# FFT filter with a bilinear layer on one core: the first transform's tiles alternate between two sets of buffers

## The chip, the cores and the metric

One core of a Trainium2 chip. The time is the device time of one execution, in microseconds (us); the number for the kernel before is the median of three runs.

## The reference

```python
X = np.fft.rfft(x, axis=1)              # x: (8, 3072, 256)
Y = X * (filt_r + 1j * filt_i)[None]
y = np.fft.irfft(Y, n=3072, axis=1)
t = y.reshape(8 * 3072, 256)
return (t @ w_a) * (t @ w_b) @ w_out    # 256 -> 1536 -> 256
```

Eight batches of 3072 positions by 256 channels are filtered in the frequency domain along the positions, and each position then goes through a bilinear layer.

## The kernel before, in words

**The mathematics.** The transform of length 3072 = 128 x 24 is done in four steps of small matmuls: a first transform over 128 positions for each of 24 residues (`s1`, lines 355 to 365, two residues a step, so 12 steps a batch), a second over the 24 with the filter (`s2`, `cross`, `sum_y`, `split_y`, lines 412 to 443, 16 steps a batch), an inverse over 24 (`is1`, line 445), and an inverse over 128 (`is2`, line 544, two calls for each of six chunks of a batch). Between the steps the data goes through DRAM: the first transform stores `zh` and `zl` (`store_z`, lines 367 to 372, three DMAs a step from step 8 on, two before), the filter step loads `zt` (line 398), `is1` stores `td`, and `load_t` (line 537) loads `tt` and `gt`.

**Precision.** Operands are split in a rounded high part and a rest, and a product is made of three matmuls (high by high, high by low, low by high). The split of a tile is always the same pair of instructions: ScalarE (ACT) casts into the high part, and GpSimd (POOL), or VectorE (DVE) where the source is in PSUM, subtracts it to get the low part. For the first transform these are `xh` and `xl` (lines 351, 352, from the loaded `xt`) and `zh` and `zl` (lines 363, 364, from PSUM).

**The main loop and its slots.** `pair` (line 611) is the bilinear layer for two blocks of 128 hidden features: seven products by a Strassen-like scheme (`term`, 6 matmuls each, lines 582 to 584, in the PSUM tiles ps_p, ps_q, ps_r), copies of partial sums by ACT (`held_sum`, line 623), sums by DVE (line 627), the product g (lines 649, 652, 661), its split into gh and gl (`parts`, lines 590, 591) and the output projection (`project`, 24 matmuls a pair, lines 601 to 603). Without other work a pair is 66 matmuls. There are 6 pairs a chunk and 36 a batch. In a pair there are two places, called slots here, at which other work is put in: `hooks(plan, 2p)` ahead of term 3 and `hooks(plan, 2p+1)` behind term 4. So a batch has 72 slots, and while batch b is in the bilinear layer, its slots carry the transforms of batch b+1. The order on every engine is the order in which the program issues the instructions.

**What stands in which slot.** For batch 0, while it makes the first transform of batch 1, a step i begins in slot 12 + i: the split of x in slot 13 + i, the matmuls `s1` in slot 14 + i, `store_z` in slot 15 + i. So each of the slots 15 to 25 holds, in this order, the store of one step, `s1` of the next with the load of a table, the split of x of the one after it, and a load of x two steps ahead:

```python
at(t + 1 if b == 0 else t + 2, split_x, b + 1, i)
    at(t + 1 if b == 0 else t + 2, load_x, b + 1, i + 2)
at(t + 2 if b == 0 else t + 3, s1, b + 1, i)
at(t + 3 if b == 0 else t + 4, store_z, b + 1, i)
```

In the later batches a step begins in every second slot (t = 2i). Slots 17 and 19 of batch 0 also hold `is2` (lines 548 to 557), slot 20 also `load_t` and the first `x_parts`, slot 21 the second (`x_parts`, lines 566, 567, splits the input of the bilinear layer into xoh and xol). The filter steps begin in slot 29 in every batch.

**Buffers.** The tiles of the first transform and of the filter step come from one pool, `later`, each under a tag of its own: xh, xl, zh, zl with one buffer each, xt and st with two, yh, yl, y, v with one each. All of xh, xl, zh, zl, yh, yl, y and v have the same size, 128 x 512 elements of four bytes. An instruction that writes a tile waits until everything has been done that reads the tile before it in the same buffer; for zh and zl those readers are the DMAs of `store_z`. All DMAs named here are issued on the queue of SP, in the program's order.

Of the kernel before, what the change touches and what calls it, by code (L numbers as in the profile page):

```python
# [10 lines left out]
F32R = mybir.dt.float32r  # L11
# [7 lines left out]
B, S, D, DFF = 8, 3072, 256, 1536  # L19
# [177 lines left out]
def fft_filter_bilinear_kernel(ctx: ExitStack, tc, x, filt, fny, wa, wb, wo, s1c, gc, fc, fl, ic, sc, s1f, ff, fi, out):  # L197
# [14 lines left out]
    later, moe = [], []  # L212
# [129 lines left out]
    def load_s(b, i):  # L342
        st = later[0].tile([128, 2, 2, 128], F32R, name="st", tag="st", bufs=2)
        nc.sync.dma_start(out=f32(st), in_=s1d[i])
        held["s", b, i] = st

    def split_x(b, i):
        xt = held.pop(("x", b, i))
        xh = later[0].tile([128, 2, D], F32R, name="xh", tag="xh", bufs=1)
        xl = later[0].tile([128, 2, D], F32R, name="xl", tag="xl", bufs=1)  # L350
        nc.scalar.copy(out=xh, in_=xt)
        nc.gpsimd.tensor_tensor(out=xl, in0=xt, in1=f32(xh), op=ALU.subtract)
        held["xs", b, i] = xh, xl

    def s1(b, i):
        (xh, xl), st = held.pop(("xs", b, i)), held.pop(("s", b, i))
        ps = ps_f.tile([128, 2, D], F32, name="ps", tag="ff")
        for n in range(2):
            for q, (w, m) in enumerate(((0, xh), (0, xl), (1, xh))):
                nc.tensor.matmul(ps[:, n], st[:, n, w], m[:, n], start=q == 0, stop=q == 2)  # L360
        zh = later[0].tile([128, 2, D], F32R, name="zh", tag="zh", bufs=1)
        zl = later[0].tile([128, 2, D], F32R, name="zl", tag="zl", bufs=1)
        nc.scalar.copy(out=zh, in_=ps)
        nc.vector.tensor_tensor(out=zl, in0=ps, in1=f32(zh), op=ALU.subtract)
        held["zs", b, i] = zh, zl
# [305 lines left out]
    with tc.manual_schedule():  # L671
# [60 lines left out]
        for b in range(B):  # L732
# [14 lines left out]
            if b + 1 < B:  # L747
# [5 lines left out]
                for i in range(NI):  # L753

                    t = o + i if b == 0 else 2 * i
                    at(t + 1 if b == 0 else t + 2, split_x, b + 1, i)
                    if i + 2 < NI:
# [3 lines that stand above are left out]
                    if i + 2 < NI:  # L761
                        at(t + 2 if b == 0 else t + 3, load_s, b + 1, i + 2)
                t = 26 if b == 0 else 28
# [4 lines left out]
                for i in range(NJ):  # L768
                    t = 29 + 2 * i
# [8 lines left out]
            for c in range(NC):  # L778
                nb, ncx = (b, c + 1) if c + 1 < NC else (b + 1, 0)
                if nb < B:  # L780
                    t = 12 * c + 5 if c + 1 < NC else 67
# [60 lines left out]
```

## Time and profile before

| | us |
|---|---|
| median of 3 runs | 2687.28 (2687.25 to 2687.7) |
| the profiled execution | 2686.96 |
| its span, first to last instruction | 2685.2 |
| TensorE (PE) busy | 2590.9 (96%) |
| VectorE (DVE) busy | 1667.8 (62%) |
| ScalarE (ACT) busy | 1411.5 (53%) |
| GpSimd (POOL) busy | 1321.5 (49%) |
| mean granted TensorE clock | 0.984 of 2.4 GHz |

A row of a timeline gives the start, the duration, the engine, the line of the kernel, the operation and its tiles; in brackets stands how long the engine had been idle before it and what ended the idle time. A row of waits gives the engine and line that waited, what it waited for, the sum in us, how often, and the longest. Matmuls overlap: each is shown with some 0.28 us, but they start about 0.12 us apart.

### The profile page before, as it was taken

To read this page: it belongs to the slowest core of one execution; us is meant where nothing else is said; L and a number is where in the kernel's file an instruction comes from. 1 tells how busy PE (TensorE), PEld (TensorE's weight loads), DVE (VectorE), ACT (ScalarE), POOL (GpSimd) and SP (SyncE) were. 2 spreads that over 40 slices of the span, in tenths; PEclk is the share of its full clock that TensorE was granted. 3 is DMA by queue.
4 is the path that set the end of the run, shared out by engine and by line. 5 is a ranking of instruction groups with operands and counts; after the bars stand their busy time and mean duration, and the time that the engine had idled before them with its cause. 6 is when DMAs were issued, how large, how long until landed. Compare 5 with 4: busy or idle time off the path is not lost.

```text
span 2685.2 us, 54082 instructions
## 1 busy us (share of the span) xinstructions
PE 2590.9 (96%) x20920; PEld 2521.5 (94%) x20920; DVE 1667.8 (62%) x2648; ACT 1411.5 (53%) x2630; POOL 1321.5 (49%) x1044
## 2 busy tenths in 40 slices
PE   4687999999999999999999999999999999999999
PEld 2387999999999999999999999999999999999999
DVE  5773686457855588456874578654885558744443
ACT  3454455555555555555555555555555555544444
POOL 3564454554545455455544545454454545534333
PEclk6899999999999999999999999999999999999999
DMA  7624442345423443244432444134441444311000
GB/s 247 179 97 156 158 145 70 111 138 153 139 64 123 153 140 108 77 135 159 137 93 83 156 144 141 53 127 155 135 130 61 138 147 143 97 39 32 29 21 17
DMA packets 213635, 310.88 MB, mean 116 GB/s; under 512 B 21393, under 2 KB 121298, under 8 KB 213330
## 3 DMA queue, kind: packets, MB, share of 16 engines
q1 hardware_dynamic: 184882, 278.85, 32.6%
q10 hardware_dynamic: 28496, 28.58, 3.5%
q8 instruction: 164, 2.69, 0.4%
q14 instruction: 93, 0.76, 0.1%
HBM read 202.49 MB, written 108.00 MB: 116 GB/s over the span
## 4 chain that ended last, share of the span: by engine, by line
PE 87%; POOL 4%; DVE 3%; DMA 3%; issue 2%; ACT 1%; SPq 0%; ACTq 0%; POOLq 0%; DVEq 0%
PE po L603 10%; PE ps_p L582 9%; PE ps_p L584 9%; PE ps_p L583 9%; PE po L601 9%; PE po L602 9%; PE ps_r L584 5%; PE ps_r L582 5%; PE ps_r L583 5%; PE ps L548 3%; PE ps_q L582 2%; PE ps_q L584 2%; PE ps_q L583 2%; PE ps L360 2%; PE ps L407 2%
## 5 line engine op out<-in xcount | busy, mean ns | idle before, releaser
L591 POOL TENSOR_TENSOR gl<-g,gh 128x512 fp32r<-128x512 f32 x576 | 748.4, 1299 | 959.0 <-ACT gh L590 891.1
L601 PE MATMUL po<-woh,gh 128*128 128x256 f32 x2304 | 656.9, 285 | 0.0
L603 PE MATMUL po<-woh,gl 128*128 128x256 f32 x2304 | 650.4, 282 | 3.1 <-POOL gl L591 1.1
L590 ACT CAST gh<-g 128x512 fp32r<-128x512 f32 x576 | 359.0, 623 | 551.0 <-DVE g L649 527.4
L602 PE MATMUL po<-wol,gh 128*128 128x256 f32 x2304 | 646.5, 281 | 0.0
L627 DVE TENSOR_TENSOR cs<-ps_r,s 128x512 f32<-128x512 f32 x288 | 199.1, 691 | 448.5 <-PE ps_r L584 395.0
L623 ACT COPY s<-ps_p 128x512 f32<-128x512 f32 x576 | 338.0, 587 | 240.4 <-PE ps_p L584 203.8
L603 PEld LDWEIGHTS po<-woh,gl 128*128 128x128 f32 x2304 | 434.3, 188 | 7.8 <-POOL gl L591 7.8
L601 PEld LDWEIGHTS po<-woh,gh 128*128 128x128 f32 x2304 | 435.8, 189 | 3.1
L602 PEld LDWEIGHTS po<-wol,gh 128*128 128x128 f32 x2304 | 435.5, 189 | 2.9
L582 PE MATMUL ps_p<-xoh,wah 128*128 128x256 f32 x1152 | 326.9, 284 | 29.9 <-ACT s L623 16.5
L584 PE MATMUL ps_p<-xol,wbh 128*128 128x256 f32 x1152 | 324.2, 281 | 0.0
L583 PE MATMUL ps_p<-xoh,wal 128*128 128x256 f32 x1152 | 323.9, 281 | 0.0
L584 PE MATMUL ps_p<-xol,wah 128*128 128x256 f32 x1152 | 323.4, 281 | 0.0
L582 PE MATMUL ps_p<-xoh,wbh 128*128 128x256 f32 x1152 | 323.0, 280 | 0.0
L583 PE MATMUL ps_p<-xoh,wbl 128*128 128x256 f32 x1152 | 322.8, 280 | 0.0
L627 DVE TENSOR_TENSOR cs<-ps_q,s 128x512 f32<-128x512 f32 x288 | 199.1, 691 | 182.9 <-PE ps_q L584 158.5
L649 DVE TENSOR_TENSOR g<-cs 128x512 f32<-128x512 f32 x288 | 301.3, 1046 | 5.6 <-POOL gl L591 5.6
L567 POOL TENSOR_TENSOR xol<-xf,xoh 128x256 fp32r<-128x256 f32 x192 | 245.7, 1300 | 21.3 <-ACT xoh L566 21.3
L661 DVE TENSOR_TENSOR g<-ps_p,cs 128x256 f32<-128x256 f32 x288 | 122.1, 424 | 213.9 <-ACT cs L660 211.2
L442 POOL TENSOR_TENSOR yl<-y,yh 128x512 fp32r<-128x512 f32 x112 | 144.2, 1288 | 223.8 <-ACT yh L441 223.8
L582 PEld LDWEIGHTS ps_p<-xoh,wah 128*128 128x128 f32 x1152 | 217.5, 189 | 33.1 <-ACT s L623 18.2
(125 smaller groups left out, 6241.5 us busy)
## 6 DMA issues: line engine op xcount, KB each, us to landing
filt<-in_filt SPq DMA_DIRECT2D x336, 128.0 KB, 2.8
z<-zh SPq DMA_DIRECT2D x112, 256.0 KB, 2.9
zt<-z SPq DMA_DIRECT2D x112, 256.0 KB, 3.0
td<-t ACTq DMA_DIRECT2D x128, 192.0 KB, 2.2
out<-ot SPq DMA_DIRECT2D x95, 256.0 KB, 2.1
tt<-td SPq DMA_DIRECT2D x47, 512.0 KB, 4.2
xt<-in_x SPq DMA_DIRECT2D x84, 256.0 KB, 2.8
st<-s1d SPq DMA_DIRECT2D x84, 256.0 KB, 3.4
```

The source lines that it names most:

```text
L567: nc.gpsimd.tensor_tensor(out=xl[:, o], in0=xf[:, i], in1=f32(xh[:, o]), op=ALU.subtract)
L582: nc.tensor.matmul(o, wh[:, p, w], xh[:, i], start=first and h == 0, stop=False, skip_group_check=True)
L583: nc.tensor.matmul(o, wl[:, p, w], xh[:, i], start=False, stop=False, skip_group_check=True)
L584: nc.tensor.matmul(o, wh[:, p, w], xl[:, i], start=False, stop=True, skip_group_check=True)
L590: nc.scalar.copy(out=gh, in_=g[:, f])
L591: nc.gpsimd.tensor_tensor(out=gl, in0=g[:, f], in1=f32(gh), op=ALU.subtract)
L601: nc.tensor.matmul(o, gh[:, ts], woh[:, n], start=n == 0 and j % 2 == 0, stop=False, skip_group_check=True)
L602: nc.tensor.matmul(o, gh[:, ts], wol[:, n], start=False, stop=False, skip_group_check=True)
L603: nc.tensor.matmul(o, gl[:, ts], woh[:, n], start=False, stop=n == NF - 1, skip_group_check=True)
L623: nc.scalar.copy(out=s, in_=bank)
L627: nc.vector.tensor_tensor(out=cs[:, :, n], in0=bank, in1=s, op=ALU.add)
L649: nc.vector.tensor_tensor(out=g[:, 0].rearrange("p (t n) -> p t n", t=2), in0=cs[:, 0, 0:2], in1=cs[:, 1, 0:2], op=ALU.mult)
```

## The change

The four tiles of a step of the first transform are taken from the tags xh, xl, zh, zl when i is even and from yh, yl, y, v, the tags of the filter step, when i is odd. Nothing else is changed: the same instructions and DMAs in the same order, and the same tags with the same number of buffers in the pool.

```diff
+    SHARED = ("xh", "xl", "zh", "zl"), ("yh", "yl", "y", "v")
+
     def split_x(b, i):
         xt = held.pop(("x", b, i))
-        xh = later[0].tile([128, 2, D], F32R, name="xh", tag="xh", bufs=1)
-        xl = later[0].tile([128, 2, D], F32R, name="xl", tag="xl", bufs=1)
+        xh, xl = (later[0].tile([128, 2, D], F32R, name=n, tag=t, bufs=1) for n, t in zip(("xh", "xl"), SHARED[i % 2][:2]))
...
-        zh = later[0].tile([128, 2, D], F32R, name="zh", tag="zh", bufs=1)
-        zl = later[0].tile([128, 2, D], F32R, name="zl", tag="zl", bufs=1)
+        zh, zl = (later[0].tile([128, 2, D], F32R, name=n, tag=t, bufs=1) for n, t in zip(("zh", "zl"), SHARED[i % 2][2:]))
```

## Rows read from the trace of the kernel before

**Rows 1.** Busy time by stretches: us, busy us of each engine, clock, DMA share, GB/s.
```profile
195.00:285.00 90.00, 73.42 (x569) 71.80 (x567) 33.72 (x58) 39.22 (x77) 38.94 (x31) 0.94 0.51 166
285.00:375.00 90.00, 88.45 (x721) 86.89 (x722) 69.77 (x103) 48.84 (x92) 42.84 (x33) 1.00 0.45 138
```
**Rows 2.** Costliest groups of TensorE, 206.2 to 286.9 us: busy, mean ns | idle before.
```profile
L582 PE MATMUL ps_p<-xoh,wah 128*128 128x256 f32 x24 | 8.1, 336 | 18.0 <-ACT s L623 13.3 <-DVE cs L627 4.8
```
**Rows 3.** Waits of ACT, 206 to 287 us; the whole execution gives the same row.
```profile
ACT zh L363 <- DMA z<-zh: 29.2, 9, 5.1
```
**Rows 4.** Timelines of ACT, POOL and SP's queue, one step of the first transform.
```profile
222.42 0.58 ACT L363 CAST zh<-ps 128x512 fp32r<-128x512 f32 x1 [3.46 <-DMA z<-zh]
...
223.60 1.27 POOL L352 TENSOR_TENSOR xl<-xt,xh 128x512 fp32r<-128x512 f32 x1 [4.16 <-ACT xh L351]
...
224.89 0.38 SPq L339 DMA_DIRECT2D xt<-in_x  x1
225.33 0.46 SPq L369 DMA_DIRECT2D z<-zh  x1
...
228.81 0.58 ACT L363 CAST zh<-ps 128x512 fp32r<-128x512 f32 x1 [2.31 <-DMA z<-zh]
```
**Rows 5.** Timeline of TensorE: first transform matmul, first stall, last stall.
```profile
206.22 0.28 PE L360 MATMUL ps<-xh,st 128*128 128x256 f32 x1
...
213.93 0.28 PE L584 MATMUL ps_r<-xol,wbh 128*128 128x256 f32 x1
217.37 0.38 PE L582 MATMUL ps_p<-xoh,wah 128*128 128x256 f32 x1 [3.16 <-ACT s L623]
...
286.46 0.40 PE L582 MATMUL ps_p<-xoh,wah 128*128 128x256 f32 x1 [1.67 <-ACT s L623]
```
**Rows 6.** Busy time by stretches, columns as in rows 1, where the clock falls.
```profile
226.00:230.00 4.00, 4.00 (x23) 4.00 (x23) 1.00 (x2) 1.69 (x5) 1.28 (x2) 0.58 0.84 259
258.00:266.00 8.00, 5.66 (x36) 5.66 (x37) 2.60 (x5) 4.99 (x10) 5.63 (x5) 0.79 0.39 122
274.00:278.00 4.00, 4.00 (x23) 4.00 (x24) 0.49 (x1) 1.63 (x4) 1.88 (x2) 0.61 0.77 260
```
**Rows 7.** Timeline of TensorE: the matmuls of one is2 call.
```profile
239.34 1.06 PE L548 MATMUL ps<-gt,tt 128*128 128x128 f32 x8
```
**Rows 8.** Timelines of ACT and TensorE in slot 14, whose cast waits for no DMA.
```profile
207.13 0.59 ACT L363 CAST zh<-ps 128x512 fp32r<-128x512 f32 x1 [0.34 <-PE ps L360]
...
209.77 0.31 PE L582 MATMUL ps_p<-xoh,wah 128*128 128x256 f32 x1
```
**Rows 9.** Timelines of ACT and SP's queue around slot 20, step 6.
```profile
247.91 0.59 ACT L363 CAST zh<-ps 128x512 fp32r<-128x512 f32 x1 [2.30 <-DMA z<-zh]
...
251.80 0.43 SPq L369 DMA_DIRECT2D z<-zh  x1
...
257.66 0.58 ACT L363 CAST zh<-ps 128x512 fp32r<-128x512 f32 x1 [5.08 <-DMA z<-zh]
```
**Rows 10.** Timeline of POOL in slot 20.
```profile
250.33 2.43 POOL L567 TENSOR_TENSOR xol<-xf,xoh 128x256 fp32r<-128x256 f32 x2
```
**Rows 11.** Two stretches as in rows 1, and landing of the DMAs of zh.
```profile
206.20:286.90 80.70, 62.66 (x477) 61.04 (x476) 30.34 (x52) 33.58 (x67) 33.45 (x27) 0.94 0.54 173
...
270.00:280.00 10.00, 7.42 (x51) 7.22 (x49) 3.04 (x5) 4.29 (x8) 3.61 (x3) 0.83 0.66 219
...
DMA to landing us min/median/max: 2.4/3.4/5.8
```
**Rows 12.** Waits of TensorE from 285 us to the end.
```profile
PE ps_r L584 <- POOL xol L567: 2.5, 7, 0.4
```
**Rows 13.** Line 649 from 195 to 285 us: duration ns min/median/max.
```profile
L649 DVE TENSOR_TENSOR g<-cs x7: 681/681/1252, 200.7 to 280.1; 128x512 f32<-128x512 f32 x7
```
**Rows 14.** Timelines of SP's queue and DVE: last store of step 11, first y.
```profile
289.93 0.45 SPq L372 DMA_DIRECT2D z<-zh  x1
...
300.25 0.74 DVE L418 SCALAR_TENSOR_TENSOR y<-ps,sct,filt 128x512 f32<-128x512 f32 x1
```

## The prediction

> **What bounds the kernel now.** I read the busy time by stretches first. Before and after the first transform of batch 1 TensorE is busy nearly all the time; in 195 to 285 us it is busy 73.4 of 90 us at a mean clock of 0.94, and in the next 90 us 88.5 at 1.00 [rows 1]. So time can be won only in that stretch. Who ends TensorE's idle time there is the second view: 18.0 us before matmuls into ps_p, released by ACT's copy of s or by DVE's sums [rows 2]. Both engines take their work in order, so the third view asks what ACT itself waited for: its cast into zh waited 29.2 us, nine times, for the DMA that stores the zh of the step before [rows 3]. The whole execution has the same sum in the same nine, so the casts of the other batches, where a step comes only every second slot, wait for no store.
>
> The fourth view is one turn of the loop [rows 4]: cast zh of step 2 at 222.42, then xh of step 3, then POOL's xl from 223.60 for 1.27, then SP issues the load of x (it waits for that xl, since xt has two buffers), and only behind it on SP the store of zh at 225.33, 2.91 us after the cast. It lands when ACT goes on, at 228.81: 3.48 us. One turn is 6.39 us. TensorE's own work for one slot is shorter: 30 matmuls pass from 206.22 [rows 5] to 209.77 [rows 8], of which the last shows 0.03 of waiting, so 0.1173 us each; a pair with two transform steps has 66 + 12 = 78, so 9.15 us, 4.6 us a slot. The store's round trip sets the pace, not TensorE.
>
> **What the stage costs above TensorE's work.** From the first transform matmul (206.22) to the matmul that ends the last stall (286.46) are 80.24 us [rows 5]. Between them lie the rest of pair 7 (36 matmuls), five pairs of 66, the first 18 of pair 13 and 72 of the transform: 456 x 0.1173 = 53.5 us. Two is2 calls come to it, of about 0.95 us each (the row's 1.06 holds the tail of its last matmul) [rows 7]. That makes 55.4; the excess is 24.8 us. It has three parts: 18.0 idle [rows 2]; the clock, which falls from 2.4 to 1.2 GHz in three spells behind stalls [rows 6] and loses 0.42 x 4 + 0.21 x 8 + 0.39 x 4 = 4.9 us; and about 0.16 us at each of eight restarts (217.37 - 213.93 - 0.118 = 3.32 against 3.16 shown as idle [rows 5]), 1.3 us. 18.0 + 4.9 + 1.3 = 24.2, near the 24.8.
>
> **What the change does.** Steps with odd i take the buffers of yh, yl, y, v. No instruction or DMA is added, dropped or moved. Waits change:
>
> Removed: zh(i) no longer waits for the store of zl and zh(i-1), but for that of i-2. That store is issued 2.91 us after its cast and lands 3.48 later, 6.4 us after it [rows 4]; the next cast into the same buffer comes two slots, 9.15 us, after it. So some 2.8 us are spare. xh and xl alternate too; that is worth nothing, since xh(i) follows zh(i-1) on ACT, which waits for the matmuls that read xh(i-1).
>
> Added: the filter step's first y waits for the store of step 11, its yh for s1's matmuls five slots earlier, and step 1 of a batch for the filter step of the batch before, ten or more slots back. For y the margin is on view: last store issued at 289.93, first y at 300.25 [rows 14]; the longest landing of zh is 5.8 us [rows 11]. Queued behind that y on DVE are the pair's sums, on which TensorE waits; they cost nothing as long as those 10.3 us cover the landing. Cost 0, bounds 0 and a rival below.
>
> **What stays late.** In even slots nothing is spare: cast zh at 207.13, then zl and two sums on DVE, then term 4's matmul at 209.77, which shows 0.31 instead of 0.28 [rows 8]; a late zh passes on one for one. In odd slots the copy of s comes behind zh and xh, and TensorE has 30 matmuls, 3.5 us, before it needs that copy done. The cast of zh starts 0.9 us behind the slot's first matmul (206.22 [rows 5], 207.13 [rows 8]) and lasts about 0.6, xh and s the same, so 2.7; some 0.8 us is spare. So I look at even steps. Step 8: in the slot of step 6 the loads of tt and gt stand ahead of the store, which is issued at 251.80, 3.89 after the cast at 247.91, and lands 5.86 later [rows 9]; 9.75 against 9.15 leaves 0.6 us. Step 10: step 8 is the first whose zh is stored twice and its store comes behind a late xl; 0.4, my choice between 0 and the 2.4 us by which the longest landing exceeds the median [rows 11]. POOL: the pair with x_parts gives it two xl (1.27 each [rows 4]), two gl of much the same size and four xol, two of which take 2.43 [rows 10]: about 10.0 us in a pair of 9.15. I count 0.6 of that as reaching TensorE, about two waits of the size that TensorE has for xol elsewhere (2.5 us in 7) [rows 12]. Sum 1.6. Bounds: 0 (every wait covered), and 12 us (five even steps, each late by 2.4).
>
> **Sum.** 24.8 - 1.6 = 23.2 us. Behind the stage TensorE is at its limit [rows 1] and each later step has its place in the slots, so the gain reaches the end whole. The profiled execution took 2686.96 us, 0.3 under the median of the runs shown, 2687.28. That makes 2663.8 for it, and as a median **2664.1**. The matmul of 286.46 would come near 263.
>
> **A row that speaks against it.** Of the seven products g (L649) in the stage the longest took 1.25 us, where POOL's xol ran beside it, the others 0.68 [rows 13]. With the stalls gone POOL's work lies closer. If every pair paid this, 7 x 0.57 = 4.0 us more; I take none, since between g and the project matmuls that use it lie more than 2 us of other TensorE work. The Trainium skill, SBUF — State Buffer, section "SBUF: two separate sides", says that a DVE operation with two SBUF inputs and a GpSimd operation exclude each other for a whole instruction; by that each such meeting would be paid in full, and the 1.25 against 0.68 agrees.
>
> **Rivals.**
> (a) The DMA engines become the bound. They are busy 0.54 of 80.7 us at 173 GB/s, 14.0 MB [rows 11]. In 55.4 us that is 253 GB/s and a share of 0.78. For it: the busiest ten microseconds of the stage moved 219 GB/s [rows 11]. At that rate 14.0 MB take 64 us: gain 80.2 - 64 = 16, 2671. Against it: single 4 us stretches moved 259 and 260 [rows 6], and the engines pause in every turn now.
> (b) POOL and DVE lock each other out in every pair as above: gain 23.2 - 4.0, 2668.
> (c) The change doesn't uncouple the steps: the buffers alternate, but SP still puts each store behind the load that waits for xl, so a turn remains near 6.4 us and the stall moves from zh to another wait. For it: that order is untouched. Against it: with zh free, xl follows the matmuls, not the store. Gain 0 to 5, 2685.
> (d) Slower: y of each filter step holds DVE until the store of step 11 has landed. It decides from a landing of 10.3 us in batch 1; to eat the 23.2 us it must come 3.3 us late in each of seven batches. With one more landing of 5.8 each time, 7 x 5.8 = 41: 2664 + 41 = 2705. Against it: the load of the filter step's input already waits for that same store.
> (e) Many small waits, as in the upper bound: gain 24.8 - 12, 2674.5.
>
> **How the numbers follow.** Forecast 0.72, (a) 0.10, (b) 0.04, (e) 0.06, (c) 0.05, (d) 0.03. A change of 0.2%, 5.4 us, is about what a measurement of this kernel can tell from none. Faster: 0.72 + 0.10 + 0.04 + 0.06 = 0.92; same 0.05; slower 0.03. The range runs from the whole excess with a microsecond of reading error, 2661.5, to the bound of 12 us, 2674.5; it holds the forecast, (a), (b) and (e).
>
> **What would show it.** Right: in the changed profile ACT's wait of zh for the DMA falls from 29.2 to under 3 us; TensorE's idle time before ps_p falls from 18 to under 3; the clock stays at 1.00 through the stage; the same matmul that ended the stage at 286.46 comes near 263; the DMA share rises to about 0.78 with landings below 6 us. Wrong: landings over 6.2 us (9.15 - 2.91), a turn still near 6.4 us, or DVE waiting at y.

## The result and the profile after

The changed kernel takes 2662.84 us (median of six runs, 2660.59 to 2663.57), the kernel before 2687.2 us in the same comparison (six runs, 2683.71 to 2687.7). The ratio is 0.9911, with a 95% interval of 0.9898 to 0.9923: 24.4 us less, between 21 and 27. The forecast was 2664.1 with a range of 2661.5 to 2674.5.

The profiled execution took 2662.36 us, 24.6 less than that of before. First its busy time by stretches (us, busy us of PE, PEld, DVE, ACT and POOL, clock, DMA share, GB/s), the same stretch as in [rows 1], then the stage from its first transform matmul to the matmul that ended the last stall, as in [rows 11]:

```profile
195.00:285.00 90.00, 89.95 (x758) 89.56 (x758) 47.84 (x83) 50.95 (x97) 46.88 (x37) 1.00 0.58 194
...
205.40:261.90 56.50, 56.45 (x476) 56.15 (x475) 30.12 (x52) 34.24 (x66) 33.80 (x28) 1.00 0.74 245
```

TensorE is busy throughout and its clock never falls. The waits of TensorE from 205 us to the end, all of them:

```profile
PE ps_r L584 <- POOL xol L567: 2.5, 7, 0.4
PE po L603 <- POOL gl L591: 1.1, 2, 0.7
PE ps L405 <- DMA zt<-z: 0.2, 1, 0.2
```

The 18.0 us before ps_p [rows 2] are gone. Of ACT's nine waits of zh [rows 3] one is left (waits of ACT, 205 to 262 us):

```profile
ACT zh L363 <- DMA z<-zh: 1.1, 1, 1.1
```

One cast to the next, in the timelines of ACT and SP's queue; these are steps 2, 3 and 4, and the first and the last of them use the same buffer:

```profile
215.58 0.59 ACT L363 CAST zh<-ps 128x512 fp32r<-128x512 f32 x1 [0.84 <-PE ps L361]
...
218.53 0.46 SPq L369 DMA_DIRECT2D z<-zh  x1
...
219.88 0.58 ACT L363 CAST zh<-ps 128x512 fp32r<-128x512 f32 x1 [0.20 <-PE ps L361]
...
225.73 0.58 ACT L363 CAST zh<-ps 128x512 fp32r<-128x512 f32 x1 [0.85 <-PE ps L361]
```

The store still leaves 2.95 us behind its cast (218.53 - 215.58), as in [rows 4]. But the cast of step 3 no longer waits for it: it comes 4.30 us behind that of step 2, and what ended ACT's idle time is TensorE (PE ps L361), not a DMA. Step 4, which does need that store to have landed, comes 10.15 us behind step 2, with an is2 call in between. The ends of the stage on TensorE:

```profile
205.42 0.28 PE L361 MATMUL ps<-xh,st 128*128 128x256 f32 x1
...
261.76 0.28 PE L582 MATMUL ps_p<-xoh,wah 128*128 128x256 f32 x1
```

That is 56.34 us against 80.24 [rows 5]: 23.9 us of the 24.6. The rest lies outside the stage, which begins at 205.42 instead of 206.22. Nothing in the change touches that part, and over the profiled runs of all eleven kernels the beginning lies anywhere from 203.91 to 206.95.

### The profile page after: what moved, and what is told of

Read it like the earlier page. It is cut to its first block, busy times and chain, and to the rows that moved or that the text cites. A ratio compares the mean times of both kernels' runs of the same rounds, so it can differ in the third digit from the quotient of the medians.

```text
span 2660.6 us, 54030 instructions
## 1 busy us (share of the span) xinstructions
PE 2589.5 (97%) x20920; PEld 2518.2 (95%) x20920; DVE 1665.2 (63%) x2648; ACT 1412.2 (53%) x2630; POOL 1321.8 (50%) x1044
## 4 chain that ended last, share of the span: by engine, by line
PE 88%; POOL 4%; DVE 3%; issue 2%; DMA 2%; ACT 1%; SPq 0%; ACTq 0%; POOLq 0%; DVEq 0%
PE po L603 10%; PE ps_p L582 10%; PE ps_p L583 9%; PE ps_p L584 9%; PE po L601 9%; PE po L602 9%; PE ps_r L584 5%; PE ps_r L582 5%; PE ps_r L583 5%; PE ps L548 3%; PE ps_q L582 2%; PE ps_q L584 2%; PE ps_q L583 2%; PE ps L361 2%; POOL xol L567 2%
```

## The experiments

All comparisons are with the kernel before, run on the same chip.

**Which tiles carry the gain.** Four kernels, all from the kernel before, alternate only some of the four tiles.

The run z_only alternates zh and zl.

```diff
-        zh = later[0].tile([128, 2, D], F32R, name="zh", tag="zh", bufs=1)
-        zl = later[0].tile([128, 2, D], F32R, name="zl", tag="zl", bufs=1)
+        zh = later[0].tile([128, 2, D], F32R, name="zh", tag=("zh", "y")[i % 2], bufs=1)
+        zl = later[0].tile([128, 2, D], F32R, name="zl", tag=("zl", "v")[i % 2], bufs=1)
```

> Only zh and zl alternate (with y and v); xh and xl keep one buffer each. Theory (the whole loss is the cast into zh and the subtraction into zl waiting for the store of the step before): all of the gain, 2662 to 2665 us, ACT's waits of zh for the store about 1 us in one step. Rival (the alternation of xh and xl lets POOL and ACT run ahead and carries part of it): 5 us or more of the gain is missing, 2668 or above.

Measured: 2661.58 us, ratio 0.9912 (0.9897 to 0.9926). All of the gain.

The run x_only alternates xh and xl.

```diff
-        xh = later[0].tile([128, 2, D], F32R, name="xh", tag="xh", bufs=1)
-        xl = later[0].tile([128, 2, D], F32R, name="xl", tag="xl", bufs=1)
+        xh = later[0].tile([128, 2, D], F32R, name="xh", tag=("xh", "yh")[i % 2], bufs=1)
+        xl = later[0].tile([128, 2, D], F32R, name="xl", tag=("xl", "yl")[i % 2], bufs=1)
```

> Only xh and xl alternate (with yh and yl); zh and zl keep one buffer each. Theory: nothing, 2686 to 2688 us, ACT still waits some 29 us for the store of zh. Rival: part of the gain, 2680 or below.

Measured: 2686.51 us, ratio 1.0003 (0.9994 to 1.0012). ACT's waits in its stage (200 to 295 us) still show

```profile
ACT zh L363 <- DMA z<-zh: 26.6, 8, 4.9
```

so half of the change, the two x tiles, does nothing here.

The run zh_only alternates zh alone.

```diff
-        zh = later[0].tile([128, 2, D], F32R, name="zh", tag="zh", bufs=1)
+        zh = later[0].tile([128, 2, D], F32R, name="zh", tag=("zh", "y")[i % 2], bufs=1)
```

> Only zh alternates; zl keeps one buffer. Theory: ACT's wait goes, but DVE's subtraction into zl now waits for the store of zl, which lands half a microsecond behind that of zh. In odd slots DVE has room, in even slots it stands ahead of the sums that TensorE needs: some 1.3 us in each of six even slots, 7 to 8 us of loss left, 2668 to 2676. Rival (ACT's order alone is what hurts): the whole gain, 2663 to 2665. Second rival (both tiles have to be free for any gain): 2685 or above.

Measured: 2668.74 us, ratio 0.9939 (0.9924 to 0.9953): two thirds of the gain. Its waits from 200 to 290 us, of DVE, of ACT and of TensorE:

```profile
DVE zl L364 <- DMA z<-zl: 31.4, 10, 5.6
...
ACT s L623 <- DVE cs L627: 10.3, 4, 3.9
```

```profile
PE ps_p L582 <- ACT s L623: 6.0, 3, 2.4
PE ps_p L582 <- DVE cs L627: 3.0, 4, 1.8
```

The wait has gone from ACT to DVE in nearly its old size, and of 31.4 us on DVE 9.0 reach TensorE. The size was as expected, the place not quite: I had put all of it in even slots, by way of DVE's sums; 6.0 of it came by way of the copy of s in odd slots. That copy was late because it had to wait for a DVE sum (10.3 us in four), and the sum stood behind the late zl.

The run zl_only alternates zl alone.

```diff
-        zl = later[0].tile([128, 2, D], F32R, name="zl", tag="zl", bufs=1)
+        zl = later[0].tile([128, 2, D], F32R, name="zl", tag=("zl", "v")[i % 2], bufs=1)
```

> Only zl alternates; zh keeps one buffer. Theory: the cast of zh still waits for the store in every step and everything behind it follows, so no gain: 2684 to 2688 us. Rival (DVE's half of the wait counts for itself): 2680 or below.

Measured: 2685.69 us, ratio 0.9999 (0.9989 to 1.0008). With zh still waiting (31.6 us in ten steps on ACT) a second buffer for zl is worth nothing. So the two do not add: zl alone is worth 0, zh alone 17, both together 24.

**Where in the run the gain lies.**

The run z_batch1 alternates zh and zl in the transform of batch 1 alone.

```diff
-        zh = later[0].tile([128, 2, D], F32R, name="zh", tag="zh", bufs=1)
-        zl = later[0].tile([128, 2, D], F32R, name="zl", tag="zl", bufs=1)
+        zh = later[0].tile([128, 2, D], F32R, name="zh", tag=("zh", "y")[i % 2 if b == 1 else 0], bufs=1)
+        zl = later[0].tile([128, 2, D], F32R, name="zl", tag=("zl", "v")[i % 2 if b == 1 else 0], bufs=1)
```

> zh and zl alternate only in the transform of batch 1; the later six batches keep one buffer. Theory (all the loss is in the stage of batch 1, where a step comes every slot): the whole gain, 2662 to 2665 us. Rival (some of the gain is spread over the later batches): 2666 or above.

Measured: 2662.47 us, ratio 0.9911 (0.9897 to 0.9926). Twelve steps of one batch hold the whole gain; the other 72 steps lose nothing with one buffer.

**Is it the buffer, or the store's way to DRAM?** Two kernels move the place of the store among the slots; the second also moves the first loads of the filter step.

The run store_early is the kernel before with this edit:

```diff
-                    at(t + 3 if b == 0 else t + 4, store_z, b + 1, i)
+                    at(t + 2 if b == 0 else t + 4, store_z, b + 1, i)
```

> The kernel before, with one buffer each, but in batch 0 the store of a step is issued right behind its first transform, ahead of the loads of the table and of x of that slot, instead of behind them. Theory (what hurts is the store's whole round trip, of which 2.9 us are its place on SP's queue behind a load that waits for xl): the store leaves about 1.4 us behind the cast instead of 2.9 and the wait shrinks by 1.5 us in each of eleven steps; a turn falls from 6.4 to about 4.9 us against the 4.6 that TensorE needs. Most of the gain without a second buffer: 2664 to 2673 us. Rival (only a second buffer helps, the place on the queue is worth nothing): 2685 or above.

Measured: 2662.83 us, ratio 0.9914 (0.9899 to 0.9928). The same gain with one buffer each, more than I had expected. The timelines of ACT and SP's queue, and the landing of the DMAs of zh from 195 to 290 us (min/median/max):

```profile
210.18 0.38 SPq L339 DMA_DIRECT2D xt<-in_x  x1
...
212.00 0.59 ACT L363 CAST zh<-ps 128x512 fp32r<-128x512 f32 x1 [0.24 <-ACT cs L660]
...
212.61 0.32 SPq L369 DMA_DIRECT2D z<-zh  x1
...
216.89 0.59 ACT L363 CAST zh<-ps 128x512 fp32r<-128x512 f32 x1 [0.83 <-PE ps L360]
...
DMA to landing us min/median/max: 2.0/2.6/6.0
```

The store leaves 0.61 us behind the beginning of the cast, when the cast is just done, where I had put 1.4: nothing on SP stands ahead of it. It also lands in 2.6 us in the middle instead of 3.4 [rows 11]. I put that down to the load of x, which is issued 2.43 us before the store here and 0.44 us before it in [rows 4]; no run changes this alone. 0.6 + 2.6 = 3.2 us fits into a slot of 4.6, and ACT waited for the store only 2.8 us in two steps. The larger wait is that of step 8: the store of step 7 leaves behind the loads of tt and gt and lands some 6.0 us later, and TensorE loses 1.35 us, its only wait in this stage (timelines of SP's queue, ACT and TensorE):

```profile
242.14 0.32 SPq L369 DMA_DIRECT2D z<-zh  x1
...
248.18 0.59 ACT L363 CAST zh<-ps 128x512 fp32r<-128x512 f32 x1 [2.37 <-DMA z<-zh]
...
250.79 0.39 PE L582 MATMUL ps_p<-xoh,wah 128*128 128x256 f32 x1 [1.35 <-DVE cs L627]
```

The run store_late is the changed kernel with this edit:

```diff
-                    at(t + 3 if b == 0 else t + 4, store_z, b + 1, i)
+                    at(t + 4, store_z, b + 1, i)
...
-                t = 26 if b == 0 else 28
+                t = 28
```

> The changed kernel, two sets of buffers, but in batch 0 each store is issued one slot later (and the first loads of the filter step two slots later, as in all other batches). Theory (the pace is set by the time from a cast to the landing of its store against the time to the next cast into the same buffer): the store now leaves behind the load of x of the slot after, 2.9 us behind the next cast, lands 3.5 later, and the cast two steps on cannot come before: a turn of 6.4 us a step, as in the kernel before, so nearly the whole gain is lost: 2683 to 2689 us. Rival (two buffers are enough, wherever the store stands): 2663 to 2666.

Measured: 2685.73 us, ratio 0.9999 (0.999 to 1.0009). Two sets of buffers, and nothing is left of the gain. ACT's timeline has the old turn, 6.27 and 6.28 us from cast to cast:

```profile
229.66 0.58 ACT L363 CAST zh<-ps 128x512 fp32r<-128x512 f32 x1 [3.97 <-DMA z<-zh]
235.93 0.58 ACT L363 CAST zh<-ps 128x512 fp32r<-128x512 f32 x1 [2.15 <-DMA z<-zh]
242.21 0.59 ACT L363 CAST zh<-ps 128x512 fp32r<-128x512 f32 x1 [1.64 <-DMA z<-zh]
```

Not all of the loss is this turn, though. From the first transform matmul (203.91) to the matmul that stood at 286.46 before (here 278.69) are 74.78 us, against 80.24 in the kernel before and 56.34 in the changed kernel: 18.4 of the 23.9 us are lost in the stage. The rest is lost behind it, where TensorE waits 3.73 us for the load of the filter step's input and then runs at half clock for some 6 us, which costs 3.1 more (timeline of TensorE, and busy time from that matmul on):

```profile
278.69 0.39 PE L582 MATMUL ps_p<-xoh,wah 128*128 128x256 f32 x1 [2.30 <-ACT s L623]
...
295.41 0.58 PE L405 MATMUL ps<-zt,fct 128*128 128x256 f32 x1 [3.73 <-DMA zt<-z]
...
295.41:301.70 6.29, 6.19 (x27) 5.90 (x28) 1.92 (x3) 0.62 (x2) 0.00 (x0) 0.50 0.62 185
```

No run separates what of this second wait comes from the later stores and what from the later loads of the filter step. So the turn is shown for some three quarters of the loss; that the total met the expected range owes the rest to a wait that I had not foreseen.

**Both remedies at once.**

The run both is the changed kernel with this edit:

```diff
-                    at(t + 3 if b == 0 else t + 4, store_z, b + 1, i)
+                    at(t + 2 if b == 0 else t + 4, store_z, b + 1, i)
```

> The changed kernel with the store also issued early as in the run store_early. Theory (in the changed kernel only step 8 still waits, 1.1 us in all on ACT): that wait goes, and with it 0.3 us of TensorE's time: the same as the changed kernel within 1 us, 2661 to 2664. Rival (the order on SP matters more than that, because loads of x now come later): 2665 or above.

Measured: 2662.13 us (2661.39 to 2662.63), ratio 0.991 (0.9895 to 0.9925). No cast waits for a store any more, but the time lies within the runs of the changed kernel. No wait of TensorE is left in the stage, which takes 55.98 us here (206.53 to 262.51).

**How much room have the DMA engines?**

The run extra_stores is the changed kernel with two more stores a step in batch 1, to a scratch tensor that nothing reads:

```diff
+    junk = drc.tile([128, 4 * NI, D], F32, name="junk")
...
+        if b == 1:
+            for k in range(2):
+                nc.sync.dma_start(out=junk[:, 4 * i + 2 * k:4 * i + 2 * k + 2], in_=f32(zh))
```

> The changed kernel with two more stores of zh to a place of its own in each of the twelve steps of batch 1, 6.3 MB on top of 14.0 in the stage of 56 us; the stores lengthen the time that zh is held. Theory (the DMA engines, at a share of 0.74 and 243 GB/s in the stage, have little room left): 20.3 MB at some 290 to 320 GB/s take 63 to 70 us, so the stage grows by 7 to 14 us: 2670 to 2677. Rival (the engines still have ample room, the double buffer hides it): 2663 to 2665.

Measured: 2667.81 us, ratio 0.9931 (0.9915 to 0.9948): 5 us slower than the changed kernel, so neither side's range held it. Its waits of ACT and TensorE in the stage, TensorE's two stalls, and four stretches of busy time (columns as above):

```profile
ACT zh L364 <- DMA junk<-zh: 5.2, 2, 3.3
...
PE ps_p L586 <- DVE cs L631: 3.0, 2, 2.3
...
219.29 0.39 PE L586 MATMUL ps_p<-xoh,wah 128*128 128x256 f32 x1 [0.74 <-DVE cs L631]
251.52 0.38 PE L586 MATMUL ps_p<-xoh,wah 128*128 128x256 f32 x1 [2.25 <-DVE cs L631]
```

```profile
210.00:220.00 10.00, 9.26 (x79) 9.06 (x78) 4.46 (x8) 5.16 (x11) 5.17 (x4) 1.00 0.92 315
225.00:235.00 10.00, 10.00 (x87) 10.00 (x86) 5.72 (x11) 5.73 (x12) 5.01 (x5) 1.00 0.91 308
...
245.00:255.00 10.00, 7.75 (x53) 7.55 (x53) 3.43 (x7) 3.48 (x7) 5.98 (x5) 0.84 0.98 356
247.00:251.00 4.00, 2.27 (x20) 2.07 (x18) 1.42 (x3) 1.10 (x2) 2.29 (x3) 1.00 1.06 401
```

At 308 GB/s and a share of 0.91 TensorE still ran without a stall. The double buffer did not cover the store at two places: in 210 to 220 us, at a share of 0.92, which cost TensorE 0.74 us, and where the loads of tt and gt came on top, at a share of 0.98, which cost it 2.25 us and the clock (0.16 x 10 = 1.6 us). Together that is 4.6 of the 5 us. So in the changed kernel, at 245 GB/s, the DMA engines are not the bound. The Trainium skill, DMA: Bandwidth & Descriptors, section "Specifications", gives some 358 GB/s as the limit of a core's DRAM traffic. The 356 of these ten microseconds lies next to it, but four of them, 247 to 251 us, moved 401 GB/s, so it is not a ceiling in this trace.

## Why the prediction was right

**The place and the mechanism.** A store's round trip per step against TensorE's work per slot: shown from three sides. It goes with a second buffer (z_only), it goes with an earlier store and one buffer (store_early), and 18.4 of the 23.9 us come back with two buffers and a later store (store_late). What counts is the time from a cast to the landing of its store, against the time to the next cast into that buffer; the number of buffers only sets the second of the two.

**The size.** Excess before 80.24 - 55.4 = 24.8, now 56.34 - 55.4 = 0.9. The forecast left 1.6. Its three terms: step 8, put at 0.6, is the one cast that still waits, as forecast, behind the loads of tt and gt (timelines of SP's queue, ACT and TensorE, steps 6 and 8):

```profile
239.80 0.43 SPq L369 DMA_DIRECT2D z<-zh  x1
...
244.38 0.28 PE L361 MATMUL ps<-xh,st 128*128 128x256 f32 x1
...
245.56 0.59 ACT L363 CAST zh<-ps 128x512 fp32r<-128x512 f32 x1 [1.10 <-DMA z<-zh]
...
247.82 0.28 PE L603 MATMUL po<-woh,gl 128*128 128x256 f32 x1
248.15 0.39 PE L582 MATMUL ps_p<-xoh,wah 128*128 128x256 f32 x1
```

The store landed 5.76 us after issue (5.86 in [rows 9]). Of the 1.10 us that ACT stood idle, most would have been spent waiting for TensorE anyway (0.84 and 0.85 in steps 2 and 4, shown above): the cast starts 1.18 us behind the slot's first matmul (244.38) instead of 0.9, so the store made it some 0.3 us late. TensorE's next term 4 starts 0.33 us behind the matmul before it instead of 0.12. That is 0.2 to 0.3 us against 0.6. Step 10 (0.4) and POOL (0.6) cost nothing that shows as a wait of TensorE.

The 0.9 is also not all waiting. The run both, in which no cast waits for a store, takes 55.98 us for the same matmuls, so the 55.4 was some 0.6 us too low and the waits left are about 0.4 us where 1.6 was put in. The two errors partly cancel: 23.9 us were gained in the stage against 23.2 forecast, and that they come this close is in part luck. The median of the runs fell by 24.4.

**The parts of the excess.** That the 4.9 us of lost clock would come back with the idle time is borne out: 1.00 in all of the stage.

**The x tiles.** Put at nothing, because xh follows the cast of zh on ACT: x_only shows nothing.

**Rivals.** (a) The DMA share rose to 0.74, forecast 0.78, TensorE waited for nothing, and the landing of zh did not grow (DMAs of zh from 205 to 262 us):

```profile
DMA to landing us min/median/max: 2.9/3.3/5.8
```

(b) Seven products g in the stage (195 to 265 us), the longest 1.08 us where before it was 1.25 [rows 13]. What ran beside the long one this time is POOL's xl of step 9; the product that met xol had begun 0.02 us ahead of it and kept its 0.68 (timelines of DVE and POOL):

```profile
L649 DVE TENSOR_TENSOR g<-cs x7: 681/682/1076, 199.9 to 257.3; 128x512 f32<-128x512 f32 x7
```

```profile
238.30 0.68 DVE L649 TENSOR_TENSOR g<-cs 128x512 f32<-128x512 f32 x1
238.32 2.70 POOL L567 TENSOR_TENSOR xol<-xf,xoh 128x256 fp32r<-128x256 f32 x2
...
247.25 1.29 POOL L353 TENSOR_TENSOR xl<-xt,xh 128x512 fp32r<-128x512 f32 x1
248.01 1.08 DVE L649 TENSOR_TENSOR g<-cs 128x512 f32<-128x512 f32 x1
```

The rule of the Trainium skill (SBUF — State Buffer, "SBUF: two separate sides") was not seen to be paid by TensorE: one product g in seven is long, as before, and no wait of TensorE is listed in the stage.

(c) SP's order is indeed as it was, with each store behind the load that waits for xl. It did no harm, as xl no longer waits for a store. But I had treated that order as a given; store_early shows that it was the other half of the cause, and that moving one line removes it.

(d) The first y of a filter step did not wait: DVE's only idle time before line 418 in the whole run is for the load of the filter step's input.

```profile
L418 DVE SCALAR_TENSOR_TENSOR y<-ps,sct,filt x112: 740/742/752, 275.4 to 2312.6; 128x512 f32<-128x512 f32 x112
its engine sat idle before it (us, times) until:
  DMA zt<-z: 0.2, 1
```

What was not tried is a second buffer of their own for zh and zl, so the sharing with the filter step is shown to be free only by the absence of waits.

## What to carry to other kernels

Where a tile is written, stored and written again in a loop, compare two times: from the write to the landing of its store, with the store's place on the issuing queue in it, and from the write to the next write into the same buffer. If the first is longer, the loop runs at the pace of the store, as it did here with TensorE idle for 18.0 us [rows 2]; an earlier issue shortens the first, another buffer lengthens the second, and either was enough here. Tiles that are written in the same step and leave by DMA (here zh and zl) have to be treated together: a second buffer for zl alone gained nothing, for zh alone two thirds.

## What had not been expected of the hardware

The clock does not follow from the length of a stall alone. In the kernel before, the first stall of 3.16 us [rows 5] left it at full speed, and a later one of 2.38 us did not. In the run zh_only, stalls of up to 2.38 us and 9.0 us in all never lowered it; in extra_stores one of 2.25 us did. Busy time by stretches of the kernel before behind its first two stalls, then TensorE's second stall, and the stretch of zh_only that holds all of its stalls:

```profile
218.00:222.00 4.00, 4.00 (x36) 4.00 (x36) 0.04 (x1) 0.90 (x2) 1.44 (x2) 1.00 0.63 200
222.00:230.00 8.00, 5.62 (x35) 5.42 (x34) 3.82 (x7) 3.18 (x7) 2.55 (x3) 0.79 0.52 163
...
224.98 0.39 PE L582 MATMUL ps_p<-xoh,wah 128*128 128x256 f32 x1 [2.38 <-DVE cs L627]
```

```profile
200.00:290.00 90.00, 80.98 (x671) 79.46 (x671) 41.05 (x72) 46.43 (x89) 43.65 (x34) 1.00 0.57 188
```

So the price of a stall of some 2 to 3 us can be that stall alone or that and some 1.7 us more (0.42 x 4 [rows 6]), and the 3.73 us of store_late cost 3.1 more; a forecast has to carry both cases.
